# On-chip copies of q, k and the probabilities issued from GpSimd's DMA queue

## The chip, the cores and the metric

The kernel runs on one core of a Trainium2 chip. The metric is the device time of one execution in microseconds (us). Before the change, three runs took 909.13, 910.15 and 910.55 us; the median is 910.15 us. The profile comes from one more execution, which took 909.33 us, of which 907.5 us lie inside the traced span.

## The reference

Three stages follow each other. `q`, `k` and `v` have 4 batches, 8 heads, 576 positions and 64 features; `D` below is 64.

```python
scores = (1.0 / np.sqrt(D)) * np.matmul(q, k.transpose(0, 1, 3, 2))
rel = pos[:, None] - pos[None, :]
scores = np.where((rel >= 0) & (rel < 64), scores, -1000000000.0)
attn = np.exp(scores - max); attn = attn / (sum + 1e-09)
x = (attn @ v) as 2304 tokens x 512
xn = x / sqrt(mean(x * x) + 1e-06) * rms_g
x = (silu(xn @ w_gate) * (xn @ w_val)) @ w_out        # 512 -> 1536 -> 512
h = x @ w_in2; out = (h / (1 + exp(-1.702 * h))) @ w_out2   # 512 -> 2048 -> 512
```

## The kernel before

Everything is in 32-bit precision. TensorE works on a rounded form of it (fp32r), and each large operand is split into a rounded high part and a remainder, so that a product takes three matmuls. The 2304 tokens form 18 attention tiles of 128 tokens and 6 blocks of 384 tokens (three attention tiles each).

From the start to about 85 us an order written out by hand covers the first two blocks' attention (tiles 0 to 5) and the first block's gated MLP; there the instructions keep the program's order. From then to about 290 us the half of the gated MLP that is done token block by token block runs for blocks 1 to 5, with the attention of tiles 6 to 17 woven into it. A counter advances with each matmul of the MLP (`tick`, line 125), and pieces of attention are issued at given counts (`score_at`, line 571). After that come the other half of the gated MLP and the second MLP, which have no attention in them. TensorE's instructions keep the program's order throughout. The order on the other engines and on the DMA queues is set by a planner when the program is built: it runs the program with its own durations and lets each engine take what is ready in that model, and the chip then follows that order in each queue strictly, each instruction waiting for what it needs.

One attention tile m goes as follows. `load_one` (line 296) loads q and k of the tile from HBM into a `qkv` buffer, of which there are four. For m from 7 on (`MOVED_FROM`) a second DMA copies each of the two, 256 KB, from that buffer into a part of a buffer called `moved`, of type fp32r; that makes the transposes on TensorE cheaper, and it frees the `qkv` buffer. `att_Tk` and `att_Tq` (lines 359, 365) transpose the copies on TensorE into `ps_k` and `ps_q`. `att_S` (line 379) multiplies them, VectorE reduces and masks, ScalarE takes exponentials, VectorE divides by the sum (line 432), and then the probabilities `p` are copied by DMA into `moved` too: one copy of 512 KB for even m, two of 256 KB for odd m. `att_PT` (line 442) transposes them, and `att_PV` (line 454) multiplies them by v. When `att_PV` of a tile is done, its v buffers are free, and the loads of a later tile's k and q go into them; the copies of k and q in turn free the buffers for the next v loads.

After each third tile `rms_sum` (line 482) sums squares on TensorE, VectorE adds the epsilon (`rv`, line 491), GpSimd raises the result to the power of -1/2 (`ry`, line 492), and `rms_spread` (line 497) uses it on TensorE, in the product `ps_r<-ident,ry`. These are the only instructions of GpSimd in the woven stage.

All DMAs but one small one are issued by SyncE (SP), in one queue: loads, stores, weights and the copies into `moved` (by `dma`, line 134).

Of the kernel before, what the change touches and what calls it, by code (L numbers as in the profile page):

```python
# [9 lines left out]
F32 = mybir.dt.float32  # L10
# [31 lines left out]
def window_attention__gated_mlp__mlp_kernel(  # L42
# [13 lines left out]
    nc = tc.nc  # L56
# [44 lines left out]
    def runs(t0, n):  # L101
        done = 0
        while done < n:
            b, s = divmod(t0 + done, S)
            step = min(n - done, S - s)
            yield done, step, b, s
            done += step
# [6 lines left out]
    def on_pe(op, *args, **kw):  # L114
        ins = op(*args, **kw)  # L115
        if pinned[0]:
            tc.keep_in_program_order(ins)
        return ins
# [11 lines left out]


    starting = [True]

    def dma(**kw):
        ins = nc.sync.dma_start(**kw)
        if starting[0]:
            tc.keep_in_program_order(ins)
# [51 lines left out]
    def after(ins):  # L189
        return tc.issue_after(ins) if ins is not None else nullcontext()  # L190
# [89 lines left out]
    def part_tile():  # L280
        if not quad:
            pool = qp if n_quads[0] < 3 else wr
            n_quads[0] += 1
            t = pool.tile([128, 4, 512], F32, tag="w", name="quad")
            quad.extend(t[:, i, :] for i in range(4))
        return quad.pop(0)
# [4 lines left out]
    def moved_tile(m):  # L291
        if m not in moved:
            moved[m] = qp.tile([128, 4, 512], F32R, tag="w", name="moved")
        return moved[m]

    def load_one(i):
        kind, m = ld_order[i]
        ld_next[0] = max(ld_next[0], i + 1)
        if i < N_FIRST:
            t = part_tile().rearrange("p (h d) -> p h d", h=H)  # L300
        else:
            t = at.tile([128, H, D], F32, tag="qkv", name="qkv", bufs=NLD)
        ld_tile[kind, m] = t
        if kind == "v":
            if m == 0:
                nc.vector.memset(t[64:128], 0.0)
                rr = [(0, 64, 0, 0)]
            elif m % 4 == 0:
                rr = [(64 * e, 64) + divmod((m - e) * GB, S) for e in range(2)]
            else:  # L310
                rr = list(runs((m - 1) * GB, 128))
        else:
            rr = list(runs(m * 128, 128))
        src = {"q": q, "k": k, "v": v}[kind]
        for off, n, b, s in rr:
            dma(out=t[off:off + n], in_=src[b, :, s:s + n, :].rearrange("h s d -> s h d"))
        if kind != "v" and m >= MOVED_FROM:
            part = moved_tile(m)[:, "kq".index(kind), :]
            dma(out=part.bitcast(F32), in_=t.rearrange("p h d -> p (h d)"))
            ld_tile[kind, m] = part.rearrange("p (h d) -> p h d", h=H)  # L320
            ld_done.add((kind, m))

    def load_some():
        while ld_next[0] < len(ld_order) and ld_order[ld_next[0] - NLD] in ld_done:
            load_one(ld_next[0])
# [9 lines left out]
    def att_bank(kind, m=None):  # L335
        shape = [128, 512]
        if m is not None and m < T0 // 128:
            if kind in "kq":
                return acc_p.tile(shape, F32, tag="acc" + "23"[kind == "q"], name="ps_" + kind)
            if kind in "r":  # L340
                return acc_p.tile(shape, F32, tag="acc%d" % m, name="ps_r")
            if kind == "v":
                return mm_p.tile(shape, F32, tag="gv"[m % 2], name="ps_v")
        return atp.tile(shape, F32, tag="att", name="ps_" + kind)
# [31 lines left out]
    def key_blocks(n):  # L376
        return slice(0, 4, 3) if n % 4 == 0 else slice((n - 1) % 4, (n - 1) % 4 + 2)

    def att_S(m):
        QT = qts[m]  # L380
        banks = [att_bank("s") for _ in range(2)]
        prev = last_pt[0]
        for hp in range(NHP):
            for g, e in ((0, 0), (0, 1), (1, 0), (1, 1)):
                with after(prev):
                    prev = on_pe(
                        nc.tensor.matmul,
                        banks[e][64 * g:64 * g + 64, hp * 128:(hp + 1) * 128],
                        QT[64 * e:64 * e + 64, hp, 64 * g:64 * g + 64],
                        KT[64 * e:64 * e + 64, hp, key_blocks(2 * m + g), :],  # L390
                        start=True,
                        stop=True,
                    ).ins
        first = next((g for g in range(2) if (2 * m + g) % GPB == 0), None)
        mask = masks[:, MASKS.index(((m + 1) % 2, first))].rearrange("p a b -> p (a b)")
        sm = at.tile([128, 3, 2 * NHP], F32, tag="sm", name="sm", bufs=6)
        whole = m % 2 == 0
        if whole:
            pp = at.tile([128, 2 * NHP, 128], F32, tag="p", name="p", bufs=1)
            p = [pp[:, e * NHP:(e + 1) * NHP, :] for e in range(2)]  # L400
        else:
            p = [at.tile([128, NHP, 128], F32, tag=f"p{e}", name="p") for e in range(2)]
        for e in range(2):
            for hp in range(NHP):
                i = e * NHP + hp
                nc.vector.tensor_tensor_reduce(  # L406
                    p[e][:, hp, :],
                    banks[e][:, hp * 128:(hp + 1) * 128],
                    mask,
                    op0=ALU.add,  # L410
                    op1=ALU.min,
                    scale=-0.125,
                    scalar=3e38,
                    accum_out=sm[:, 0, i:i + 1],
                )
            for hp in range(NHP):
                i = e * NHP + hp
                last_exp[0] = nc.scalar.activation(  # L418
                    p[e][:, hp, :],
                    p[e][:, hp, :],  # L420
                    AF.Exp,
                    bias=sm[:, 0, i:i + 1],
                    scale=-1.0,
                    accum_out=sm[:, 1, i:i + 1],
                ).ins
        r = sm[:, 2, :]
        nc.vector.tensor_scalar(r, sm[:, 1, :], SUM_EPS, None, ALU.add)
        nc.vector.reciprocal(r, r)
        part = moved_tile(m + 1)[:, 2:4, :]
        for e in (0,) if whole else (0, 1):  # L430
            src, rr = (pp, r) if whole else (p[e], r[:, e * NHP:(e + 1) * NHP])
            norm_ins = nc.vector.tensor_tensor(
                src, src, rr.unsqueeze(2).to_broadcast([128, rr.shape[1], 128]), ALU.mult
            )
            hold_v[0] = norm_ins.ins
            if whole:
                dma(out=part.bitcast(F32), in_=pp.rearrange("p (e h) t -> p e (h t)", e=2))
            else:
                dma(out=part[:, e].bitcast(F32), in_=src.rearrange("p h t -> p (h t)"))
        p_tiles[m] = [part[:, e, :].rearrange("p (h t) -> p h t", h=NHP) for e in range(2)]  # L440

    def att_PT(m, parts=(0, 1)):
# [130 lines left out]
    for m in range(2 * m0, N_ATT + 1):  # L573
        t = score_at[m - 2 * m0]
# [20 lines left out]
    if True:  # L595
        nc.scalar.dma_start(out=g_sb, in_=rms_g.rearrange("(k p) -> p k", p=128))
        for i in range(N_FIRST):
            load_one(i)
# [308 lines left out]
        def run_step(name):  # L907
            key, n = re.match(r"([A-Za-z]+)(.*)", name).groups()
            if key in ("Lk", "Lq", "Lv"):
                m = int(n)  # L910
                for kind, i in [("v", 2 * m), ("v", 2 * m + 1)] if key == "Lv" else [(key[1], m)]:
                    load_one(ld_order.index((kind, i)))
# [603 lines left out]
        for sb in range(1, NSB):  # L1516
# [28 lines left out]
            if sb + 1 < NSB:  # L1545
# [3 lines left out]
                src = lambda e, sb=sb: x2d[sb + 1][:, :, e * TB:(e + 1) * TB]  # L1549
# [36 lines left out]
```

## Time and profile before

| | |
|---|---|
| median of three runs | 910.15 us (909.13 to 910.55) |
| profiled execution | 909.33 us, span 907.5 us |
| TensorE matmuls (PE) | 898.2 us busy, 99% of the span |
| VectorE (DVE) | 602.9 us, 66% |
| ScalarE (ACT) | 508.2 us, 56% |
| GpSimd (POOL) | 12.9 us, 1% |
| SP's DMA queue (q1) | 158800 packets, 238.97 MB, 78.4% of 16 engines |

PE is busy in nearly the whole span, at the full granted clock. SPq stands for SP's issuing of DMAs; the time at such a row is that of the issue, and the transfer lands later. PEld is the load of a weight tile into TensorE, which comes just before the matmul.

### The profile page before, as it was taken

The page shows a single profiled execution, that of the slowest core. Times are in us where ns is not written, and L with a number is a line of the kernel's source. Part 1 is how long each engine was busy: PE and PEld are TensorE (multiplying, and loading weights), DVE is VectorE, ACT ScalarE, POOL GpSimd, SP SyncE. Part 2 cuts the span into 40 slices and gives each one's busy share as a digit, 9 for nine tenths or more (in the row PEclk, how much of TensorE's full clock was granted, in tenths as well). Part 3 has the DMA queues.
Part 4 walks back from the last instruction along what each step waited for, and adds up shares of the span by engine and source line. Part 5 has one row for each costly group of instructions (what it writes and reads, how often), then busy time and mean ns, then how long its engine had stood idle before and what let it go on. Part 6 is the DMA issues. An engine that isn't in the chain of part 4 may idle for free.

```text
span 907.5 us, 16653 instructions
## 1 busy us (share of the span) xinstructions
PE 898.2 (99%) x6458; PEld 867.8 (96%) x6458; DVE 602.9 (66%) x1237; ACT 508.2 (56%) x1026; POOL 12.9 (1%) x39
## 2 busy tenths in 40 slices
PE   9999999999999999999999999999999999999998
PEld 8999999899999999999999998889899999999998
DVE  5998657767779747937867896656633488234753
ACT  6896656647375447626726657565545455245442
POOL 2000000000000000000000000000000000000000
PEclk9999999999999999999999999999999999999999
DMA  9987577678948868569979989898697788777851
GB/s 205 255 239 212 171 183 219 200 234 259 267 134 317 325 229 313 226 198 360 358 257 355 401 308 384 318 324 296 204 353 262 279 285 309 240 260 261 322 206 53
DMA packets 159407, 240.04 MB, mean 264 GB/s; under 512 B 81248, under 2 KB 131424, under 8 KB 155744
## 3 DMA queue, kind: packets, MB, share of 16 engines
q1 hardware_dynamic: 158800, 238.97, 78.4%
q8 instruction: 51, 0.84, 0.4%
q14 instruction: 28, 0.23, 0.1%
q10 hardware_dynamic: 528, 0.00, 0.0%
HBM read 167.64 MB, written 59.24 MB: 250 GB/s over the span
## 4 chain that ended last, share of the span: by engine, by line
PE 90%; DMA 5%; DVE 2%; ACT 2%; issue 0%; SPq 0%; DVEq 0%; ACTq 0%
PE acc L115 21%; PE psa L115 18%; PE psb L115 13%; PE acca L115 7%; PE psv L115 6%; PE psg L115 6%; PE accb L115 5%; DMA moved<-qkv 2%; PE ps_warm L121 2%; PE psg L121 1%; PE acc L121 1%; PE psv L121 1%; PE ps_v L115 1%; DMA qkv<-in_k_dram 1%; PE ps_s L115 1%; DMA wh<-whi 1%
## 5 line engine op out<-in xcount | busy, mean ns | idle before, releaser
L115 PE MATMUL psa<-xop,wt 128*128 128x384 f32 x1008 | 192.9, 335 | 0.9 <-ACT sn L1038 0.8
L115 PEld LDWEIGHTS psa<-xop,wt 128*128 128x128 f32 x1008 | 176.5, 188 | 4.2 <-ACT sn L1038 1.1
L115 PE MATMUL psb<-xop,wt 128*128 128x384 f32 x756 | 147.0, 335 | 0.3 <-ACT a L1492 0.3
L115 PEld LDWEIGHTS psb<-xop,wt 128*128 128x128 f32 x756 | 132.6, 188 | 2.7 <-ACT a L1492 0.8
L1042 DVE TENSOR_TENSOR sn<-sn,psb 128x384 f32<-128x384 f32 x84 | 46.3, 551 | 69.2 <-PE psb L115 67.9
L115 PE MATMUL acc<-g,w 128*128 128x384 f32 x432 | 78.1, 334 | 0.0
L115 PEld LDWEIGHTS acc<-g,w 128*128 128x128 f32 x432 | 75.2, 188 | 0.0
L115 PE MATMUL acca<-wo,sop 128*128 128x256 f32 x576 | 72.0, 283 | 0.3 <-DVE sop L1394 0.3
L1394 DVE TENSOR_TENSOR sop<-g,sop 128x768 fp32r<-128x768 f32 x56 | 53.2, 955 | 28.6 <-ACT sop L1393 28.5
L1038 ACT COPY sn<-psa 128x384 f32<-128x384 f32 x84 | 39.9, 475 | 56.9 <-PE psa L115 56.9
L115 PEld LDWEIGHTS acca<-wo,sop 128*128 128x128 f32 x576 | 70.8, 191 | 0.5 <-DVE sop L1394 0.5
L1393 ACT CAST sop<-g 128x768 fp32r<-128x768 f32 x56 | 46.4, 836 | 40.4 <-PE accb L115 23.1
L115 PE MATMUL acc<-whi,g 128*128 128x512 f32 x192 | 67.8, 393 | 0.0
L1370 ACT ACTIVATE g<-sn 128x384 f32<-128x384 f32 x48 | 25.2, 526 | 51.8 <-DVE sn L1042 51.8
L115 PE MATMUL accb<-wo,sop 128*128 128x256 f32 x432 | 52.8, 283 | 0.0
L115 PEld LDWEIGHTS accb<-wo,sop 128*128 128x128 f32 x432 | 52.3, 192 | 0.0
L115 PE MATMUL acc<-ah,w 128*128 128x384 f32 x240 | 50.8, 342 | 0.0
L1001 ACT CAST xop<-xr 128x768 fp32r<-128x768 f32 x42 | 33.9, 835 | 29.3 <-DVE xr L999 25.4
L115 PE MATMUL psv<-xh,w 128*128 128x384 f32 x240 | 50.3, 340 | 0.0
L115 PE MATMUL psg<-xh,w 128*128 128x384 f32 x240 | 50.0, 342 | 0.1
L418 ACT ACTIVATE p<-p,sm 128x128 f32<-128x128 f32 x96 | 37.2, 390 | 17.1 <-DVE sm L406 17.1
L115 PEld LDWEIGHTS acc<-ah,w 128*128 128x128 f32 x240 | 41.4, 188 | 1.7 <-issue 1.0
(204 smaller groups left out, 1564.1 us busy)
## 6 DMA issues: line engine op xcount, KB each, us to landing
wt<-wh SPq DMA_DIRECT2D x48, 896.0 KB, 6.7
wo<-wp SPq DMA_DIRECT2D x28, 1024.0 KB, 6.2
st<-in_moe_w_out_dram SPq DMA_DIRECT2D x28, 512.0 KB, 7.9
wt<-wg SPq DMA_DIRECT2D x14, 896.0 KB, 7.3
wt<-wv SPq DMA_DIRECT2D x14, 896.0 KB, 7.7
xr<-x SPq DMA_DIRECT2D x12, 768.0 KB, 6.5
wh<-whi SPq DMA_DIRECT2D x8, 896.0 KB, 8.7
wh<-m SPq DMA_DIRECT2D x8, 896.0 KB, 9.4
```

The source lines that it names most:

```text
L115: ins = op(*args, **kw)
L121: ins = op(*args, **kw)
L418: last_exp[0] = nc.scalar.activation(p[e][:, hp, :], p[e][:, hp, :], AF.Exp, bias=sm[:, 0, i:i + 1], scale=-1.0, accum_out=sm[:, 1, i:i + ...
L1001: nc.scalar.copy(t[:, 0], src)
L1038: nc.scalar.copy(t, ps[:, :TB])
L1042: nc.vector.tensor_tensor(t, t, ps[:, :TB], ALU.add)
L1370: hold[0] = nc.scalar.activation(g[pg, q][:, j % 2], c, AF.Gelu_apprx_sigmoid).ins
L1393: nc.scalar.copy(t[:, 0], src)
L1394: nc.vector.tensor_tensor(t[:, 1], src, t[:, 0].bitcast(F32), ALU.subtract)
```

## The change

All 22 copies of q and k and all 18 copies of probabilities into `moved` are issued by GpSimd instead of SP. Their sources, destinations and sizes stay, and so do all other transfers.

```diff
+    def hop(**kw):
+        nc.gpsimd.dma_start(**kw)
+
     def dma(**kw):
         ins = nc.sync.dma_start(**kw)
...
         if kind != "v" and m >= MOVED_FROM:
             part = moved_tile(m)[:, "kq".index(kind), :]
-            dma(out=part.bitcast(F32), in_=t.rearrange("p h d -> p (h d)"))
+            hop(out=part.bitcast(F32), in_=t.rearrange("p h d -> p (h d)"))
...
             if whole:
-                dma(out=part.bitcast(F32), in_=pp.rearrange("p (e h) t -> p e (h t)", e=2))
+                hop(out=part.bitcast(F32), in_=pp.rearrange("p (e h) t -> p e (h t)", e=2))
             else:
-                dma(out=part[:, e].bitcast(F32), in_=src.rearrange("p h t -> p (h t)"))
+                hop(out=part[:, e].bitcast(F32), in_=src.rearrange("p h t -> p (h t)"))
```

## Rows read from the trace of the kernel before

**Rows 1.** What PE waited for: total us, times, longest us.
```profile
PE ps_q L115 <- DMA moved<-qkv: 1.6, 1, 1.6
PE ps_k L115 <- DMA moved<-qkv: 1.2, 1, 1.2
```

**Rows 2.** Woven stage: PE, PEld, DVE, ACT, POOL busy us; PE clock, DMA share, GB/s.
```profile
79.00:290.00 211.00, 208.15 (x1895) 196.23 (x1894) 148.95 (x449) 122.65 (x342) 4.50 (x5) 1.00 0.72 217
```

**Rows 3.** Issues of the copies: count, issue ns min/median/max, first and last start us.
```profile
L135 SPq DMA_DIRECT2D moved<-qkv x22: 470/471/1055, 79.8 to 237.8; - x22
L135 SPq DMA_DIRECT2D moved<-p x18: 472/533/2330, 97.4 to 267.8; - x18
```

**Rows 4.** Chain of waits before the first PE wait: start us, us, what.
```profile
171.67 8.41 DMA moved<-qkv
```

**Rows 5.** Order of time on SP there: start us, us, engine line op.
```profile
171.18 0.39 SPq L1165 DMA_DIRECT2D wg<-m  x1
...
172.76 7.72 SPq L135 DMA_DIRECT2D qkv<-in_v_dram  x3
```

**Rows 6.** Chain of waits before the second PE wait.
```profile
223.62 4.60 DMA moved<-qkv
```

**Rows 7.** Order of time on SP there.
```profile
218.94 4.44 SPq L135 DMA_DIRECT2D st<-in_moe_w_val_dram  x3
```

**Rows 8.** Tile 10's copies of k and q: their issue on SP, in order of time.
```profile
122.80 0.52 SPq L135 DMA_DIRECT2D moved<-qkv  x1
...
124.69 0.47 SPq L135 DMA_DIRECT2D moved<-qkv  x1
```

**Rows 9.** The copy of q in the view of its tile, issue to landing.
```profile
DMA to landing us min/median/max: 2.3/2.3/2.3
```

**Rows 10.** Order of time on PEld: tile 10's transposes of k and q.
```profile
126.25 0.49 PEld L115 LDWEIGHTS ps_k<-ident_r,moved 128*128 128x128 f32 x4
...
127.32 0.49 PEld L115 LDWEIGHTS ps_q<-ident_r,moved 128*128 128x128 f32 x4
```

**Rows 11.** Order of time on POOL, 80 to 236 us; in brackets, idle before.
```profile
80.54 1.10 POOL L789 TENSOR_TENSOR ry<-rv,mhalf 128x3 f32<-128x3 f32 x1 [47.52 <-DVE rv L121]
133.69 0.85 POOL L492 TENSOR_TENSOR ry<-rv,mhalf 128x3 f32<-128x3 f32 x1 [52.05 <-DVE rv L491]
183.12 0.85 POOL L492 TENSOR_TENSOR ry<-rv,mhalf 128x3 f32<-128x3 f32 x1 [48.57 <-DVE rv L491]
235.52 0.85 POOL L492 TENSOR_TENSOR ry<-rv,mhalf 128x3 f32<-128x3 f32 x1 [51.55 <-DVE rv L491]
```

**Rows 12.** Order of time on PEld: where the power's result is used.
```profile
83.44 0.36 PEld L121 LDWEIGHTS ps_r<-ident,ry 128*128 128x128 f32 x2
...
135.72 0.36 PEld L115 LDWEIGHTS ps_r<-ident,ry 128*128 128x128 f32 x2
...
185.15 0.59 PEld L115 LDWEIGHTS ps_r<-ident,ry 128*128 128x128 f32 x4
...
237.55 0.59 PEld L115 LDWEIGHTS ps_r<-ident,ry 128*128 128x128 f32 x4
```

**Rows 13.** Order of time on SP: tile 11's copy of q, tile 17's load of q.
```profile
135.86 0.47 SPq L135 DMA_DIRECT2D moved<-qkv  x1
...
231.56 1.11 SPq L135 DMA_DIRECT2D qkv<-in_q_dram  x1
```

**Rows 14.** That load of tile 17 in the view of its tile.
```profile
DMA to landing us min/median/max: 6.0/6.0/6.0
```

**Rows 15.** Order of time on SP, 236 to 240 us.
```profile
237.77 0.47 SPq L135 DMA_DIRECT2D moved<-qkv  x1
238.34 1.34 SPq L1165 DMA_DIRECT2D wg<-m  x1
```

**Rows 16.** Order of time on DVE, 234 to 236 us.
```profile
234.14 0.95 DVE L1159 TENSOR_TENSOR m<-m,whi 128x768 fp32r<-128x768 f32 x1
235.28 0.16 DVE L491 TENSOR_SCALAR rv<-ps_r 128x3 f32<-128x3 f32 x1 [0.19 <-PE ps_r L115]
```

## The prediction

> **What bounds the kernel now.** I read the page's first part first: PE is busy in 898.2 of 907.5 us, so a change of the DMA queues can win only what PE waits, about 9 us, and can lose whatever new waits it brings to PE. Then the view of PE's waits: the only two that a copy into `moved` ends are 1.6 and 1.2 us, one each [rows 1]. That is the whole of what the change can win directly, 2.8 us or 0.3%. The table by stretches shows the stage in which the copies run: PE 208.15 of 211 us, the clock at its higher level (1.00 of full speed), GpSimd busy for 4.50 us only, the DMA engines for 72% [rows 2]. The chain of waits then shows why the two waits arise. The first copy takes 8.41 us to land [rows 4], because it was issued 0.1 us behind a store of converted weights [rows 5]; the second takes 4.60 us [rows 6], behind three weight loads whose issue alone took 4.44 us [rows 7]. A copy with little ahead of it takes 2.3 us [rows 8, 9]. Last I read GpSimd's order of time, since the change puts 40 instructions into its queue: it has one short power per three attention tiles [rows 11], and TensorE uses its result soon after [rows 12].
>
> **What the change does, part by part.** All sums are against the profiled execution, 909.33 us, which is 0.82 us below the median of 910.15; I add the difference of the sum to the median.
>
> *The two waits go: -2.8 us.* The copies no longer stand behind the weights in SP's queue. Their sources had landed by the time of issue, so the late part of 8.41 and 4.60 us is what lay ahead of them. If a copy on its own queue lands within 5 us of the first issue and 3.2 us of the second, both waits of rows 1 are gone; a bare copy needs 2.3. What comes next on PE is MLP matmuls whose operands are long there, so no other wait takes the place. Bounds: 0 (the engines that carry the data are the same 16 and are as full as before) and -2.8. I take -2.8. This is where a rule bears on the sum. The Trainium skill (DMA: Bandwidth & Descriptors, section "Queues, rings and completion order") says that each DMA engine takes turns between the queues that have work for it, packet by packet; by that a copy shares with the backlog and doesn't stand behind it, which gives the -2.8. The row of 8.41 us fits it as far as one queue goes; for two queues no row here shows it.
>
> *The issue itself.* On SP a copy's issue takes 0.47 us, at the most 2.33 [rows 3]. GpSimd has no DMA in this trace. I bound its time per copy, d, by those two rows, and take 1.0 us, nearer to GpSimd's own shortest work of that width, 0.85 us [rows 11]. By the Trainium skill (same page, section "Specifications") the first byte comes after about 1 us from GpSimd and 0.6 us from SP, which would put d at about 0.9, so its sum differs by 0.1 us a place. The 40 issues are 40 us of GpSimd's idle time, which hides them, except where something stands behind or a transfer is already tight.
>
> *Tight transfers: +0.2 us.* I looked for copies that land shortly before their use. The tightest without a backlog is tile 10's q: issued at 124.69, landed at 127.0 [rows 8, 9], weights loaded on PE at 127.32 [rows 10], a cover of 0.33 us. With d = 1.0 the copy lands 0.53 us later: 0.2 us of wait. Tile 10's k, issued at 122.80 [rows 8] and used at 126.25 [rows 10], has 1.1 us if it takes as long. With d = 0.47 there is no wait; with d = 2.33 the copies land 1.86 us later, 1.5 us of wait at this tile, and I put 0.6 us on all others, 2.1 us in all.
>
> *The copies of the probabilities: 0.* On SP they wait for VectorE's division at the head of the queue and hold back what stands behind them; GpSimd does that waiting now. No load of SP's ends a wait of PE [rows 1], so SP's freedom wins nothing; the copies of k and q behind them come in the same order as before, so it loses nothing.
>
> *GpSimd's powers, now in a queue with the copies: +4.85 us.* This is the added wait. A queue keeps its order, so if a copy stands ahead of a power, the power waits until the copy's source has landed. Is it so ordered? SP's order shows what the planner believed: at the end of the stage it put tile 17's copy of q ahead of the store `wg<-m` [rows 15]. On VectorE that store's operand ends at 235.09 and `rv`, which releases the power, comes after it, at 235.28 [rows 16]. So in the planner's model q's source is there before the store's, and the store's before `rv`: in GpSimd's queue both copies of tile 17 go ahead of the power. Tiles 11 and 14 stand to their powers in the same way: one product with v starts the loads and the sum of squares. Costs, by place:
> Place 1: q of tile 11 has landed at 135.86 [rows 13]; plus d 1.0 and the power's 0.85, ready at 137.7. It is loaded on PE at 135.72 [rows 12]: 2.0 us.
> Place 3: q of tile 17 was issued at 231.56 and took 6.0 us [rows 13, 14], 237.56; plus 1.85 is 239.4. Used at 237.55: 1.85 us.
> Place 2 (183.12): tile 14's loads stood on SP behind a v load that waited for the 8.41 us copy, 7.72 us for three issues [rows 5]; freed, they start several us earlier and meet the power. Between 0 (they land before it) and 2.0 (as place 1); I take the middle, 1.0.
> The power at 80.54 ends at 81.64 and is used at 83.44: 1.8 us of cover against two issues from 79.8 on; 0.
> Ends by d: with 0.47, 1.45 + 1.3 and 0 at place 2; with 2.33, 3.3 + 3.15 and 0 to 3.3 there.
>
> *The plan of the other engines.* The planner's model sees other landing times and may reorder VectorE, ScalarE and SP. PE's order is kept. PE's waits that no copy ends are 9.3 - 2.8 = 6.5 us, the start and the end of the kernel among them, so a new order can win little; I take 0, with bounds of -1 and +1.5 us as an estimate from that.
>
> Sum: -2.8 + 0.2 + 2.0 + 1.85 + 1.0 = +2.25 us: 911.6 on the profiled scale and **912.4** on that of the median.
>
> **Rivals.**
> *B, the powers go first.* If the planner orders each power ahead of the copies, only -2.8 + 0.2 us stay: 910.15 - 2.6 = 907.55. For it: on the chip the first of these powers began at 133.69 [rows 11], 2.2 us before tile 11's q was there [rows 13]; against it: rows 15 and 16, where the model's order is seen. It ends on the other side of no change, and decides at the point at which a load in the model takes longer than the sum of squares and the epsilon.
> *C, GpSimd is slow at issuing.* With d = 2.33: -2.8 + 2.1 + 3.3 + 3.15 + 1.6 = +7.35: 917.5. For it: SP's worst issue, and VectorE is busy 148.95 of 211 us in that stage. The Trainium skill (SBUF — State Buffer, section "SBUF: two separate sides") warns that GpSimd can't write its descriptors while VectorE runs in a two-port mode, and blocks until that ends; it speaks against the change, and no row here shows it. Against it: in GpSimd's rows the power takes 0.85 us in each of the three places although VectorE works around it.
> *D, the own queue doesn't shorten the landing.* The same engines carry the same bytes, and the backlog stays ahead: the two waits stay, and 0.2 + 4.85 us come on top, 915.2; or without the powers 910.35. For it: 72% DMA share; against it: the copies without backlog take 2.3 us at the same share.
>
> **How the numbers follow.** Forecast (A) 0.47, with its own range of 910 to 915; B 0.28; C 0.15; D 0.10. A measurement of this kernel can tell about 0.2%, 1.8 us, from no change. Faster by more than that (below 908.3): two thirds of B, 0.19. Slower (above 912.0): 0.26 of A's 0.47, C whole, 0.07 of D, 0.48. The same: the rest, 0.33. The range runs from 907.4, which leaves out the lower third of B, to 917.5, C's middle: about 2 in 10 are outside.
>
> **What would show it right or wrong.** In the changed kernel's view of PE's waits, the two waits on `moved<-qkv` should be gone, and up to three waits on `ry` from POOL of 1 to 2 us should stand at `ps_r`, at about 135, 184 and 236 us. GpSimd's order of time should show k, q and then the power. Its DMA rows give d. If the powers stand before the copies, B is right. If copies of tile 9, 10 and 13 show up as waits, d is larger than I took. If waits on `moved<-qkv` at 180 and 228 us stay, D is right. A time under 907 or over 918, or a change in the stage after 290 us, would mean that the cause lies in the planner's new order, which I priced at nothing.

## The result and the profile after

The changed kernel took 920.19 us (median of 4 runs, 919.17 to 923.95), the kernel before beside it 910.35 us (4 runs, 909.13 to 911.42): a ratio of 1.0111, 95% interval 1.0081 to 1.014. Timed again later (e9), it took 917.74 us against 911.42 us: 1.0082, 1.0062 to 1.0103. So it is slower, as forecast, by 6 to 10 us instead of 2.25 us, and above the range. Its profiled execution took 919.2 us.

Part 1 of its page. PE's busy time grew by 2 us, the span by 9.5 us:

```profile
span 917.0 us, 16696 instructions
...
PE 900.1 (98%) x6458; PEld 867.0 (95%) x6458; DVE 602.8 (66%) x1237; ACT 509.3 (56%) x1026; POOL 34.6 (4%) x79
```

What PE waited for (total us, times, longest us), which answers [rows 1]:

```profile
PE ps_r L115 <- POOL ry L495: 3.7, 3, 2.1
PE ps_k L115 <- DMA moved<-qkv: 2.5, 3, 0.9
...
PE ps_q L115 <- DMA moved<-qkv: 1.4, 1, 1.4
```

The two waits on `moved<-qkv`, 2.8 us, have become four, 3.9 us, and three waits on the power stand beside them. The woven stage [rows 2] shows the same in one line: PE is busy 203.32 of 211 us instead of 208.15, at the same clock.

```profile
79.00:290.00 211.00, 203.32 (x1857) 189.81 (x1856) 142.85 (x436) 120.44 (x339) 25.35 (x44) 1.00 0.72 210
```

The copies' issues and their landing, in the view of the tile `moved` (count, issue ns min/median/max, first and last start), against [rows 3]:

```profile
L135 POOL DMA_DIRECT2D moved<-qkv x22: 536/542/727, 80.6 to 243.9; - x22
L135 POOL DMA_DIRECT2D moved<-p x18: 533/536/538, 97.3 to 274.9; - x18
...
DMA to landing us min/median/max: 2.2/3.8/6.7
```

An issue costs GpSimd 0.54 us, hardly more than SP. GpSimd's order of time at the three powers [rows 11]: the power (L495) stands behind the copy of k and ahead of the copy of q.

```profile
137.21 0.55 POOL L135 DMA_DIRECT2D moved<-qkv  x1 [8.56 <-DMA qkv<-in_k_dram]
137.77 0.89 POOL L495 TENSOR_TENSOR ry<-rv,mhalf 128x3 f32<-128x3 f32 x1
138.61 0.60 POOL L135 DMA_DIRECT2D moved<-qkv  x1
...
188.36 0.54 POOL L135 DMA_DIRECT2D moved<-qkv  x1 [9.81 <-DMA qkv<-in_k_dram]
188.91 0.88 POOL L495 TENSOR_TENSOR ry<-rv,mhalf 128x3 f32<-128x3 f32 x1
...
242.46 0.55 POOL L135 DMA_DIRECT2D moved<-qkv  x1 [8.16 <-DMA qkv<-in_k_dram]
243.02 0.88 POOL L495 TENSOR_TENSOR ry<-rv,mhalf 128x3 f32<-128x3 f32 x1
```

So the power waits for k alone. The trace has k's loads landed at 136.53, 187.68 and 241.78 us; each copy of k starts 0.68 us later, its issue takes 0.54 or 0.55 us, and the power begins 0.01 or 0.02 us behind it, though `rv` was there at 135.45, 185.63 and 240.70. q's loads landed at 137.51, 188.67 and 242.78 us, 0.24 to 0.26 us ahead of each power, so these times alone would also fit a wait for q; but in the program that this kernel builds, GpSimd's instructions stand in the order k's copy, power, q's copy at all three places. TensorE takes the result at once; PEld [rows 12] (the last bracket is its idle time and what ended it):

```profile
138.71 0.41 PEld L115 LDWEIGHTS ps_r<-ident,ry 128*128 128x128 f32 x3 [1.13 <-POOL ry L495]
...
189.84 0.30 PEld L115 LDWEIGHTS ps_r<-ident,ry 128*128 128x128 f32 x2 [2.37 <-POOL ry L495]
...
243.96 0.74 PEld L115 LDWEIGHTS ps_r<-ident,ry 128*128 128x128 f32 x6 [1.14 <-POOL ry L495]
```

To place every microsecond I matched the 6458 matmuls of two executions, which come in one order, and took the differences of their start times. The table has the steps of that lag against the kernel before's first profile, in us. A column is a place in TensorE's order ("q of 10" is the transpose of tile 10's q), and a positive step is time lost there:

| profile | q of 10 | three powers | k of 13 | q of 13 | k of 15 | k of 16 | other | to 288 us | after 288 us |
|---|---|---|---|---|---|---|---|---|---|
| changed | 1.57 | 1.08, 2.32, 1.08 | 1.14 | -1.77 | 1.16 | -0.56 | 0.31 | 6.34 | 3.00 |
| changed, again (e9) | 1.51 | 0.88, 2.00, 0.70 | 0.91 | -1.77 | 0.58 | -0.28 | 0.74 | 5.29 | 1.88 |
| e2, powers first | 1.65 | 0, 0, 0 | 1.34 | -1.77 | 0.54 | 0.50 | 1.41 | 3.68 | 1.88 |
| e3, p alone moved | -0.01 | 0, 0, 0 | 0 | -0.02 | 0 | -0.41 | 1.12 | 0.70 | 2.59 |
| e4, q and k alone | 0.74 | 0.76, 1.52, 1.75 | 0.48 | -1.77 | 0.10 | 0.11 | 0.48 | 4.18 | 1.13 |
| e5, before, weights behind | 0.07 | 0, 0, 0 | 0 | -1.77 | 0 | -1.39 | 1.05 | -2.03 | 1.32 |
| e6, changed, weights behind | 1.13 | 0.70, 0, 0 | 0 | -1.77 | 0 | 0.44 | 0.31 | 0.80 | 0.27 |
| e7, both repairs | 0.74 | 0, 0, 0 | 0 | -1.77 | 0 | 0.51 | 0.24 | -0.29 | 1.15 |
| e8, before again | 0 | 0, 0, 0 | 0 | -0.54 | 0 | -0.71 | 0.14 | -1.10 | 2.44 |
| e10, e5 with p on GpSimd | 0.18 | 0, 0, 0 | 0 | -1.77 | 0 | -1.40 | 0.08 | -2.90 | 1.19 |
| e11, tiles 9, 10 on SP | 0.41 | 1.03, 1.38, 0.70 | 1.47 | -1.77 | 0.43 | -0.13 | 0.56 | 4.08 | 0.43 |

"Other" is the start and all that lies between. VectorE, ScalarE and TensorE have the same order of instructions before and after, so no new plan of these engines is in it. The tile 13 rows tell the rest. Before, SP issued k's copy at 169.93 us, then the stores `wg`, then q's copy, which landed late [rows 4, 5]:

```profile
169.93 0.52 SPq L135 DMA_DIRECT2D moved<-qkv  x1
170.55 0.54 SPq L1164 DMA_DIRECT2D wg<-whi  x1
```

Now SP, rid of the copies, runs on to the stores, and both stand ahead of k's copy. TensorE is 2.9 us late by then; measured against it, the first store goes 3.7 us earlier than before, and k's copy about at its old time. At tile 15 it is the second store `wv<-m` that gets ahead of k's copy, 1.7 us earlier against TensorE. SP's order of time:

```profile
169.75 0.90 SPq L1167 DMA_DIRECT2D wg<-whi  x1
170.74 0.38 SPq L1168 DMA_DIRECT2D wg<-m  x1
...
210.37 0.63 SPq L1167 DMA_DIRECT2D wv<-whi  x1
211.89 0.34 SPq L1168 DMA_DIRECT2D wv<-m  x1
```

and the copies of k of tiles 13 and 15, issued 2 and 1 us behind them, need 5.14 and 6.71 us in the chain of waits, where 2.3 was the bare price. They land at 178.11 and 219.88 us, 0.6 and 0.2 us after the second store of each pair (177.54 and 219.67):

```profile
172.97 5.14 DMA moved<-qkv
...
213.17 6.71 DMA moved<-qkv
```

In the view of the DMA engines from 213 to 217 us, both of tile 15's copies are issued and none of their packets moves: q1 is SP's queue, q0 GpSimd's, and q0 has no row.

```profile
q1 hardware_dynamic: 304, 1.67, 102.0%
...
issues: line engine op xcount, KB each, median us to landing
moved<-qkv POOLq DMA_DIRECT2D x2, 256.0 KB, 5.8
```

From 217 to 220 us, the stores all but through, it is q0's turn:

```profile
q0 software_dynamic: 160, 0.52, 43.2%
q1 hardware_dynamic: 24, 0.06, 4.8%
```

### The profile page after: what moved, and what is told of

Read it like the earlier page. It is cut to its first block, busy times and chain, and to the rows that moved or that the text cites. A ratio compares the mean times of both kernels' runs of the same rounds, so it can differ in the third digit from the quotient of the medians.

```text
span 917.0 us, 16696 instructions
## 1 busy us (share of the span) xinstructions
PE 900.1 (98%) x6458; PEld 867.0 (95%) x6458; DVE 602.8 (66%) x1237; ACT 509.3 (56%) x1026; POOL 34.6 (4%) x79
## 4 chain that ended last, share of the span: by engine, by line
PE 82%; DMA 8%; DVE 4%; ACT 2%; issue 2%; SPq 1%; POOL 0%; POOLq 0%; ACTq 0%; DVEq 0%
PE psa L115 18%; PE acc L115 17%; PE psb L115 13%; PE acca L115 7%; PE psg L115 5%; PE accb L115 5%; PE psv L115 5%; DMA qkv<-in_k_dram 2%; DMA moved<-qkv 2%; PE psg L121 1%; PE acc L121 1%; DMA xr<-x 1%; PE psv L121 1%; PE ps_v L115 1%; PE ps_warm L121 1%
## 5 line engine op out<-in xcount | busy, mean ns | idle before, releaser
L115 PEld LDWEIGHTS psg<-xh,w 128*128 128x128 f32 x240 | 41.4, 188 | 2.8 <-DVE a L1204 1.7
```

## The experiments

**e1: three queues side by side.** A kernel of its own, that leaves the whole computation out: one 256 KB copy from SBUF to SBUF, issued by SP, ScalarE or GpSimd, alone, behind two loads of 1 MB on SP, and with two further loads on SP after it.

```diff
+    for before, after in ((0, 0), (1, 0), (1, 1)):
+        for name in ("sp", "act", "pool"):
+            eng = {"sp": nc.sync, "act": nc.scalar, "pool": nc.gpsimd}[name]
...
+                for i, t in enumerate(ahead):
+                    fix(nc.sync.dma_start(out=t, in_=flat[:, 2048 * i:2048 * (i + 1)]))
...
+            fix(eng.dma_start(out=dst, in_=src))
...
+                for i, t in enumerate(late):
+                    fix(nc.sync.dma_start(out=t, in_=flat[:, 2048 * (2 + i):2048 * (3 + i)]))
```

> A kernel of its own that leaves the whole computation out: nine times one copy of 256 KB within SBUF, issued from SP, ScalarE or GpSimd; three times alone, three times shortly after two 1 MB loads were issued on SP, three times with two more such loads issued on SP about 1 us after the copy. Theory W (a copy on GpSimd's queue is served only when what SP issued before it has drained): alone 2.3 us from any queue, GpSimd's beginning some 0.6 us late; behind 2 MB the copy lands with or after the loads, 5 to 7 us, from all three queues. Rival S (queues share an engine packet by packet, as I predicted): SP's copy lands behind the loads, ScalarE's and GpSimd's within 3 to 4 us. Rival G (GpSimd is slow by itself): its copy alone takes 4 us or more. If GpSimd's queue has a lower rank than SP's, the two loads issued later also land before its copy; if it is first come, first served, they land after.

Each copy in the view of its destination (issue ns, then issue to landing; min is the one alone, the others stand behind 2 MB):

```profile
L43 SPq DMA_DIRECT2D dst_sp<-src x3: 470/471/509, 2.0 to 68.9; - x3
...
DMA to landing us min/median/max: 2.3/5.3/5.5
...
L43 ACTq DMA_DIRECT2D dst_act<-src x3: 472/473/491, 10.1 to 88.3; - x3
...
DMA to landing us min/median/max: 2.3/5.3/5.6
...
L43 POOL DMA_DIRECT2D dst_pool<-src x3: 536/538/670, 18.3 to 108.4; - x3
...
DMA to landing us min/median/max: 2.4/5.0/5.1
```

The three queues agree within 0.6 us in every case, and a copy behind the loads lands 0.55 to 0.7 us after the second of them (33.88 against 33.27 us from SP, 60.87 against 60.19 from GpSimd). The loads issued later land after it. So at these sizes what was issued first goes first, whichever queue it is in: W holds, sharing (S) and a slow GpSimd (G) fall. Each case ran once.

**e2: powers ahead of the copies.** In tiles 11, 14 and 17 the copies are asked for 19 ticks later and ordered behind the power.

```diff
-            hop(out=part.bitcast(F32), in_=t.rearrange("p h d -> p (h d)"))
...
+            def copy():
+                with after(last_pow[0]):
+                    hop(out=part.bitcast(F32), in_=t.rearrange("p h d -> p (h d)"))
...
+            if m in (11, 14, 17):
+                at_tick(ticks[0] + 19, lambda: (copy(), load_some()))
+            else:
+                copy()
...
+        last_pow[0] = nc.gpsimd.tensor_tensor(y, v, mhalf[:, :n], ALU.pow).ins
```

> The changed kernel with the copies of tiles 11, 14 and 17 put behind the power in GpSimd's queue; nothing else. Theory: the three waits on ry (3.7 us in the view of waits, 4.2 us by matching TensorE's instructions one by one) go, and the time falls from 920.2 by about 4.2 us to 916; the waits on moved stay. Rival (the power was late for another reason, or the copies of these tiles become late in turn): within 1.5 us of 920.

913.48 us (10 runs) where I had expected 916, ratio 1.0038 (1.002 to 1.0057). PE waits for no power now; four waits for k are left:

```profile
PE ps_k L115 <- DMA moved<-qkv: 3.6, 4, 1.7
...
PE ps_q L115 <- DMA moved<-qkv: 1.4, 1, 1.4
```

The powers are shown: their steps, 4.48 and 3.58 us in the two profiles of the changed kernel, are zero here, and the rest of the loss stays.

**e3 and e4: the two halves of the change.** The probabilities' copies alone on GpSimd, and those of q and k alone.

e3, against the changed kernel:

```diff
-            hop(out=part.bitcast(F32), in_=t.rearrange("p h d -> p (h d)"))
+            dma(out=part.bitcast(F32), in_=t.rearrange("p h d -> p (h d)"))
```

e4, against the kernel before:

```diff
+    def hop(**kw):
+        nc.gpsimd.dma_start(**kw)
...
-            dma(out=part.bitcast(F32), in_=t.rearrange("p h d -> p (h d)"))
+            hop(out=part.bitcast(F32), in_=t.rearrange("p h d -> p (h d)"))
```

> Only the 18 copies of the probabilities on GpSimd's queue, those of q and k on SP as before. Theory: no power stands behind a waiting copy, and k and q keep their place ahead of the weights in SP's queue: no wait on ry, waits on moved within 1 us of the 2.8 us of the kernel before; time within 2 us of 910.4. Rival (any use of GpSimd's queue costs, for instance by disturbing the transfers of the stage after 290 us, +2.9 us there): 913 or more, with the late waits of the changed kernel.

> Only the 22 copies of q and k on GpSimd's queue, the probabilities on SP as before. Theory: this part carries the loss: the three waits on ry (about 4 us) and the waits on moved for k of tiles 13 and 15 and q of tile 10 stay; 917 to 921. Rival (the probabilities' part matters as much, since it is what frees SP to put the weights ahead): 912 to 916, with k of tiles 13 and 15 on time.

e3: 910.26 us, ratio 1.001 (0.9991 to 1.003); no wait for a power, the two old waits as before. e4: 915.62 us, 1.0045 (1.0025 to 1.0066):

```profile
PE ps_r L115 <- POOL ry L495: 3.2, 3, 1.5
PE ps_k L115 <- DMA moved<-qkv: 1.5, 2, 1.3
```

Alone, the probabilities' copies cost nothing, and those of q and k cost 4.1 us. That is less than the changed kernel's loss and less than the 917 to 921 us that I had expected; it lies where the rival had it, 912 to 916. So most of the loss is that of q and k; beside them the probabilities' copies seem to add to it (the interval of e4, 1.0025 to 1.0066, just meets that of e9). At tiles 13 and 15 the copies of k land 0.6 us behind the second store here too (176.49 after 175.89, 216.40 after 215.79). Against TensorE this store is issued as early as in the changed kernel, but it lands 6.1 and 6.3 us after its issue instead of 6.8 and 7.8, so that PE waits less; why it lands sooner is open.

At the third power e4 has the order that I had forecast for the changed kernel, both copies ahead, and the step there is 1.75 us instead of 1.08:

```profile
239.70 1.15 POOL L135 DMA_DIRECT2D moved<-qkv  x2 [11.76 <-DMA qkv<-in_k_dram]
240.87 0.88 POOL L495 TENSOR_TENSOR ry<-rv,mhalf 128x3 f32<-128x3 f32 x1
```

**e5: the other order, without GpSimd.** The kernel before, with the weights' loads and stores ordered behind the last copy of q.

```diff
+            last_copy[0] = nc.sync.dma_start(out=part.bitcast(F32), in_=t.rearrange("p h d -> p (h d)")).ins
...
-                w_load(w_next[1] + 1)
+                with after(last_copy[0]):
+                    w_load(w_next[1] + 1)
...
+                    with after(last_copy[0]):
+                        nc.sync.dma_start(out=d[:, 0], in_=env["hi"].bitcast(F32))
+                        nc.sync.dma_start(out=d[:, 1], in_=env["t"][:, 0:7])
```

> The kernel before with all copies still on SP; the only edit puts the loads and the stores of converted weights behind the last copy of q in SP's order. Theory W (a copy lands right after what was issued ahead of it, whatever its queue): with no weights ahead the copies at about 170 and 218 us land in 2.3 to 3 us, the two waits of 1.6 and 1.2 us on moved<-qkv are gone, and the time is 2 to 2.8 us below the kernel before, about 907.5 where that is 910.2. Rival V (the transfers pushed back are needed as early as the copies): a later weight load or v load turns late, waits on w or st appear on PE or on the casts, and the time is not below that of before. Rival R (waits of this size go up in what the late stage loses anyway): the two waits go, the time stays within 0.1%.

908.54 us (12 runs), ratio 0.9982 (0.9966 to 0.9999). SP's order of time at tile 13, where before one of the two copies stood behind `wg` [rows 5]:

```profile
169.38 1.78 SPq L320 DMA_DIRECT2D moved<-qkv  x2
171.25 0.54 SPq L1167 DMA_DIRECT2D wg<-whi  x1
171.88 0.40 SPq L1168 DMA_DIRECT2D wg<-m  x1
```

Neither copy ends a wait of PE any more (the steps -1.77 and -1.39): the two waits of the forecast go by order alone. The medians show 1.8 us of it, with an interval that begins close to nothing.

**e6 and e7: the changed kernel with the weights behind, and with both repairs.** A 64-byte transfer of SP reads the landed copy and so makes SP wait for it; the weights go behind that. The planner also put two of the three powers ahead in e6. e7 adds e2's edit.

```diff
+            if kind == "q":
+                last_copy[0] = nc.sync.dma_start(out=peek[m:m + 1, :], in_=part.bitcast(F32)[0:1, 0:16]).ins
...
+                with after(last_copy[0]):
+                    w_load(w_next[1] + 1)
...
```

> The changed kernel, with the weights' loads and stores held on SP until q's copy of the tile has landed (a 64-byte transfer of SP reads the copy's result and so waits for it). Theory W: the new waits on moved<-qkv at tiles 13 and 15 (1.2 us each) and the rest of 0.6 us at tile 16 go; tile 10's 1.6 us stays, since it comes of GpSimd's start of 0.65 us behind a landed source, as does any power that still stands behind a copy (here one place of three, about 1.1 to 2.2 us). That makes 4.5 to 7 us less than the changed kernel's 920.2: 913 to 916. Theory G (what is lost is GpSimd's own slowness in issuing): the waits on moved stay at 1 us and more, and the time stays at 917 or above, less only what the two freed powers give.

> Both repairs at once: powers ahead of the copies at tiles 11, 14 and 17, and the weights held back until q's copy has landed. If the powers (4.2 us), the weights ahead of the copies (W, 3 us) and tile 10's slow start (1.6 us) are all that was lost before 290 us, only tile 10's is left, and the two waits of before are gone: 910.2 - 2.8 + 1.6 = 909, at the most 911.5 with the scatter of the late stage. If the loss after 290 us (about 3 us in the changed kernel's profile) belongs to GpSimd's queue, it stays: 912 to 914.

e6: 914.55 us (12 runs), ratio 1.0044 (1.0025 to 1.0064). e7: 912.9 us (12 runs), 1.0027 (1.0011 to 1.0044). In both the steps at tiles 13 and 15 are zero; PE's waits in e6:

```profile
PE ps_k L115 <- DMA moved<-qkv: 1.6, 1, 1.6
...
PE ps_q L115 <- DMA moved<-qkv: 0.9, 1, 0.9
...
PE ps_r L115 <- POOL ry L499: 0.4, 1, 0.4
```

The 1.6 us is tile 16, whose wait the theory wanted gone: its load of k, issued at 217.22 us, landed at 226.07, so there it is the source that is late. e7's profile stands 0.29 us below the kernel before at 288 us and 0.87 above it at the end, but its median is 2.5 us above (1.0 to 4.0). I had expected 909, at most 911.5; 912 to 914 was to mean that GpSimd's queue costs something after 288 us. The profile has 1.15 us there, less than the kernel before's own 2.44 (e8), but its execution, 910.91 us, is one of the shortest; what the others lose has no profile here, and the rival is neither shown nor excluded.

**e8 and e9: both kernels once more**, without an edit, as controls.

> The kernel before once more, unchanged, as a control: how far do two profiled executions of one program differ in the stage after 290 us? If landings there scatter by themselves (R), its matmuls drift against the first profile by steps of 0.5 to 1.5 us at about 300, 417 and 500 us, as they do in the changed kernel. If the late loss belongs to the change (L), the two profiles agree within 0.5 us to the end. The ratio of times is 1 within 0.2% either way.

> The changed kernel once more, unchanged: how much of its loss stands in every execution? If the loss is the steps before 290 us (6.2 us in its first profile) and the late steps are scatter (R, as in the two profiles of the kernel before, which differ by up to 2 us at 300 us), the steps at tiles 10, 13 and 15 and at the three powers come again within 0.5 us each, the late waits of PE sum to anything between 1.5 and 4 us, and the ratio to the kernel before is 1.006 to 1.010. If the late loss belongs to the change (L), the same steps at about 307 and 505 us come again and the ratio stays at 1.010 to 1.013.

e8: 909.68 us, ratio 0.9996 (0.9974 to 1.0017). Its PE waits have a line that the first profile of the same kernel had not:

```profile
PE psg L115 <- DVE a L1201: 1.9, 1, 1.9
...
PE ps_q L115 <- DMA moved<-qkv: 1.0, 1, 1.0
...
PE ps_k L115 <- DMA moved<-qkv: 0.5, 1, 0.5
```

After 288 us it loses 2.44 us against its own twin, as much as the changed kernel's 3.00 and 1.88; over all eleven profiles the late part goes from 0.27 to 3.00 us with no relation to the edit that I can see. So it can't be booked on the change. Before 288 us it stands 1.10 us below its twin, by the two old waits (-0.54 and -0.71), so the steps there are sure to half a microsecond or so only. e9: 1.0082; the steps before 288 us come again in the same places, 5.29 us after 6.34.

**e10: e5 with the probabilities on GpSimd.**

```diff
-                dma(out=part.bitcast(F32), in_=pp.rearrange("p (e h) t -> p e (h t)", e=2))
+                nc.gpsimd.dma_start(out=part.bitcast(F32), in_=pp.rearrange("p (e h) t -> p e (h t)", e=2))
...
```

> The kernel before with the weights held behind q's copy, as in e5, and the copies of the probabilities alone on GpSimd's queue: the part of the change that cost nothing, on top of the order that took the two waits away. If the probabilities' copies are worth nothing wherever they are issued (their row in the first sum), the two waits on moved<-qkv stay away and the time is that of e5 within 0.2%, ratio 0.996 to 1.000. If SP's freedom counts after all (loads of k and q no longer stand behind copies that wait for VectorE), it is a further 1 us or more below e5, 0.995 to 0.997. If GpSimd's queue harms by itself, PE waits on ry or on moved come back and it is above 1.001.

907.97 us (11 runs) against 911.42: ratio 0.9973 (0.9962 to 0.9984), the fastest kernel here, with no wait on `moved` or `ry`:

```profile
PE ps_v L604 <- DVE QT L601: 1.5, 1, 1.5
PE psb L115 <- ACT sn L1039: 1.1, 2, 0.7
PE psa L115 <- ACT sn L1039: 0.9, 1, 0.9
```

Its interval and that of e5 overlap, so the probabilities' queue is worth nothing that these runs can tell.

**e11: tiles 9 and 10 back on SP.**

```diff
-            hop(out=part.bitcast(F32), in_=t.rearrange("p h d -> p (h d)"))
+            (dma if m in (9, 10) else hop)(out=part.bitcast(F32), in_=t.rearrange("p h d -> p (h d)"))
```

> The changed kernel with the copies of q and k of tiles 9 and 10 alone back on SP; every engine's order but these two queues' is that of the changed kernel. Theory L (each copy of GpSimd starts 0.65 us after its source has landed, and frees the source's buffer that much later, so the loads behind it start later too): tile 10's q lands about 2 us earlier, the wait of 1.3 to 1.6 us on moved<-qkv at about 129 us is gone, and the time is 1 to 1.7 us below the changed kernel, ratio to the kernel before 1.006 to 1.009. Rival Q (the load of q itself is late, because the probabilities' copies on GpSimd's queue share the engines with it): its load takes 5.8 us as in the changed kernel, and 0.7 us or more of the wait stays.

916.23 us (4 runs), ratio 1.0078 (1.005 to 1.0106), too wide to tell a microsecond. The profile can: tile 10's wait falls from 1.4 to 0.2 us.

```profile
PE ps_q L115 <- DMA moved<-qkv: 0.2, 1, 0.2
```

The copy of q starts 0.01 us after its load has landed (125.74) and lands at 128.11; on GpSimd it started 0.65 us after (125.76, 126.41) and landed at 129.13. So GpSimd's late start, with a landing 0.4 us slower, is 1.0 us of the wait. L's other half fails: the load of q lands as late as in the changed kernel, 1.1 us after that of the kernel before (124.67). The probabilities' copies on GpSimd (rival Q) aren't the reason either, for in e4, where SP issues them, it lands at 125.65. Why, is open.

## Why the prediction was wrong

| step | forecast | first profile | second |
|---|---|---|---|
| the two waits go | -2.8 | -2.33 | -2.05 |
| other copies late (k of 13 and 15) | 0 | +2.30 | +1.49 |
| tile 10 | +0.2 | +1.66 | +1.51 |
| powers | +4.85 | +4.48 | +3.58 |
| start and the rest | 0 | +0.22 | +0.74 |
| to 288 us (the terms are rounded) | +2.25 | +6.34 | +5.29 |

*The two waits go: this step failed.* It let a copy land within 5 and 3.2 us because its own queue would take turns with the backlog, and it let no other wait take the place. The steps of -1.77 and -0.56 came, but with them +1.14 and +1.16 at k of 13 and k of 15: -0.03 in all instead of -2.8. The copies passed nothing. q of 13 was again issued behind both stores (173.92 us), and landed at 178.75, 4.8 us later and 1.2 us after the second store; it landed 1.3 us earlier than before, as the stores had gone earlier, and TensorE, held up at k of the same tile, came to it 4.1 us later. So the wait has moved from q to k, whose copy now stands behind the stores. A copy got next to nothing before what was issued ahead of it was through: no packet of q0 from 213 to 217 us, and e1 in isolation. The rule of the Trainium skill on which that sentence leaned (DMA: Bandwidth & Descriptors, section "Queues, rings and completion order": turns between queues) is not what these runs show for copies of 256 KB behind transfers of about 1 MB. Rival D, "the backlog stays ahead", had the mechanism and got 0.10; it too thought of the old two waits, not of new ones.

*"SP's freedom wins nothing, so it loses nothing": this failed with it.* The copies in SP's queue had held the weights' stores back. Without them SP issues the same stores before the copies of two tiles. I had looked for what the copies wait for, not for what waits behind the copies. Putting the stores back behind the copies removes both steps (e6, e7: 0 and 0), and doing so without GpSimd removes the old waits as well (e5).

*Tile 10: right place, the term mis-sized.* Instead of 0.2 us it is 1.6. The issue's busy time is 0.54 us, below my d of 1.0; but a copy starts 0.65 us after its source has landed, where SP needed 0.02, the landing itself took 2.72 us, and the load was 1.1 us late. The cover of 0.33 us was gone with the first of these.

*Powers: the added wait is right, its working is not, and the sum is luck.* Three waits on `ry` stand at the three places, and e2 takes all three away; 4.48 us is close to 4.85. But the forecast put the copies of both k and q ahead of each power, and only k's stands there: what [rows 15] and [rows 16] say of the planner's order did not carry over to the changed kernel. k's source lands about 1 us before q's. With k alone ahead (its loads landed at 134.87 and 236.55 us in the kernel before) the same sum gives 1.0 and 0.85 us at the outer places, where 1.08 was measured at each and 2.0 and 1.85 forecast. The middle place came to 2.32 us, above its upper end of 2.0, since tile 14's k landed only at 187.68. The two misses cancel. Rival B happened by half, each power ahead of q's copy alone; C, a slow issue, did not: 0.73 us was the longest.

*The planner: right.* The orders of the three compute engines are the same. I had said that a loss after 290 us would mean the planner; the loss is there in the first profile, and e8 shows that the kernel before has it too.

*Sum.* The steps give 6.3 and 5.3 us; the medians differ by 9.8 and 6.3, with intervals that reach from 5.6 to 12.7. The two profiles have a further 3.00 and 1.88 us after 288 us, where two profiles of the kernel before differ by 2.44 us without a change. Why the first series is slower than the second is open.

## What to carry to other kernels

Moving a transfer to another queue did not move it past what was already under way here; what counted was when it was issued against the big transfers of all queues, so order these behind the small ones that the critical engine waits for (1.8 us in e5, without a new queue). Before you take an instruction out of a queue, list what it was holding back there, since that will now start earlier. An engine that also computes for the critical path is a poor issuer of transfers that wait: whatever stands behind a copy waits for the copy's source.

## What the runs showed of the hardware

A 256 KB copy between SBUF tiles landed 2.3 us after its issue from SP and ScalarE and 2.4 us from GpSimd, and 5.0 to 5.6 us when 2 MB were issued ahead of it on SP, from all three alike. GpSimd began a copy 0.3 us after VectorE's result in e1 and 0.65 to 0.7 us after a landed load in the kernel; SP 0.01 to 0.03 us after either. GpSimd began a power 0.01 or 0.02 us after the issue of the copy ahead of it. Two profiled executions of the same kernel drifted apart by 2.44 us after 288 us; 2.07 us of it lie at one wait of TensorE, which the chain of waits follows back to the load `xr<-x`, 8.96 us long.
